# Gated linear attention with an ELU feed-forward on one core: low halves of four weight chunks by subtraction instead of matrix products, with a new start order

## The chip, the cores and the metric

The kernel runs on one core of a Trainium2 chip. The metric is the device time of one execution in microseconds (us). The engines have the names of the profile: PE (TensorE matmul), PEld (its weight load), DVE (VectorE), ACT (ScalarE), POOL (GpSimd) and SP (SyncE, which issues the loads).

## The reference

A gated linear attention runs over 4 batches x 8 heads, 768 steps, head size 48; its output is a 3072 x 384 matrix `x`, and a feed-forward with an ELU between two matrix products follows:

```python
state = alpha[t][:, None] * state + outer(k[t], v[t])
y[t]  = q[t] @ state
h = x @ w_in                     # 384 -> 2048
g = where(h > 0, h, exp(min(h, 0)) - 1)
out = g @ w_out                  # 2048 -> 384
```

The weights reach the kernel as float64, everything else as float32.

## The kernel before

**Precision.** The feed-forward's products run on pairs: each operand is kept as a rounded high part and a low part (the value less its high part), and three products (high x high, high x low, low x high) are added up in PSUM. So every weight has to be decoded, rounded (high) and subtracted (low) before it is used.

**Tiling.** Time is cut into 24 windows of 128 steps (6 to a batch), the feed-forward into 12 blocks of 256 rows (block `b` needs windows `2b` and `2b+1`) and 8 column groups `j` of 256. A weight chunk `f` is 128 x 768: `f = 2j` belongs to `w_in`, `f = 2j + 1` to `w_out`. Two chunks are decoded together as a pair `p`: chunks 0 and 2 are pair 0, 1 and 3 pair 1, 4 and 6 pair 2, 5 and 7 pair 3, and so on.

**The order.** Each piece of work is a token, a function of the same name. Two strings are walked from left to right, and each token's instructions go to the ends of their engines' queues: `START` (lines 49 to 76), which takes the kernel through the decode of all weights and up to the third column group of the feed-forward's last `O` of block 3, and `STEADY` (lines 79 to 86), which `steady()` unrolls from there. The engines run their own queues in order and wait for each other by semaphores. There is no planner at run time: what stands in the string is what each engine gets.

Tokens of a window `i`:

- `L`, `LA`, `LB`, `LV`: loads of keys, queries and decays, and of values (SP).
- `SC` (DVE scan of the decays, line 202), `LN`, `EX`, `PC` (ACT, lines 211, 216, 238), `KA`, `KB` (DVE or POOL by the tables `KAV`, `KBV`, lines 224, 229), `KC` (DVE, line 234): scaled keys. `SQ` (DVE or POOL by `SQV`, lines 251, 254): scaled queries.
- `TP` (PE transposes, line 275), `KN` (ACT copy, line 305), `S` (PE scores, line 340, from window 6 on line 324), `MK` (DVE mask), `U` and `UP` (PE, lines 387, 369, 413), `UA`, `UB`, `UC` (ACT or DVE: the state), `YL`, `Y3`, `Y` (PE, ACT, PE: the output, lines 448, 481, 493), `XH`, `XP`, `XL`, `XD`: high and low part of `x` (`XP`, for windows 0 to 2, lets PE form the rest; line 512). `ZV` is a clearing of a state buffer on POOL (line 268). `X` issues two idle products that only keep PE occupied (line 126).

Tokens of the weights: `F.f` (load, line 563), `KW.p` (ACT, line 572), `DA.p` and `DB.p` (DVE, lines 586, 591) decode a pair; `WH.f` (ACT, line 618) writes the high part. The low part is made in one of two ways. Where `f` is in the table `WPE`, `WP.f` lets PE copy the weight into PSUM by a product with the identity and take the high part off by a product with minus the identity, and `WL.f` is two ACT copies from PSUM; otherwise `WL.f` is one subtraction, on DVE where `f` is in `WLV`, else on POOL:

```python
nc.tensor.matmul(t, lhsT=ident, rhs=wm[p][:, k, c], start=True, stop=False, ...)   # WP, line 627
rest(t, wgts[f][:, 0, c])                                                          # WP, line 512
nc.scalar.copy(out=wgts[f][:, 1, h * DM:h * DM + DM], in_=t)                       # WL, line 636
eng(WLV, f).tensor_tensor(out=wgts[f][:, 1], in0=wm[p][:, k], in1=..., op=ALU.subtract)  # WL, line 638
```

`LC`, `CA`, `CB` check a weight chunk's range and are needed only at the end.

Tokens of the feed-forward: `A.b.j` (PE, 18 products, line 654; needs `WL.2j` and the `x` of block `b`), `RA`, `RB` (ACT, lines 662, 667), `RC` (DVE, line 673), `GH` (ACT, line 679), `GL` (DVE, or POOL by the table `GQS`, line 693), `O.b.j` (PE, 12 products, line 707; needs `WL.2j+1` and `GL.b.j`), `Z.b` (copy out and store).

Of the kernel before, what the change touches and what calls it, by code (L numbers as in the profile page):

```python
# [45 lines left out]
START = """
X.2.2 LA.0 SC.0 LN.0 LB.0 EX.0 KA.0 KB.0 LA.1 SC.1 KC.0 LN.1 LB.1 EX.1 SQ.1 KA.1 KB.1 TP.0 SQ.0 KC.1 S.0 PC.0 MK.0 F.2  # L50
LV.0 KN.0 U.0 UC.0 TP.1 F.0 UA.0 S.1 LV.1 LV.3 KN.1 KW.0 DA.0 DB.0 U.1 UP.1 UA.1 MK.1 YL.0 Y3.0 X.2.0 PC.1 L.2 UC.1
L.3 YL.1 SC.2 WH.0 LN.2 Y.0 SQ.2 Y3.1 XH.0 EX.2 WH.2 WP.0 F.6 Y.1 SC.3 WL.0 KA.2 KB.2 F.4 KC.2 WP.2 TP.2 XH.1 LN.3
PC.2 XP.1 KN.2 KW.2 DA.2 XP.0 DB.2 XL.0 XL.1 S.2 WL.2 EX.3 WH.6 LV.2 U.2 WH.4 UA.2 KA.3 MK.2 F.1 A.0.0 RA.0.0 A.0.1
RA.0.1 RB.0.1 UB.2 UC.2 WP.4 F.10 SQ.3 F.5 KB.3 KC.3 L.4 SC.4 RB.0.0 S.3 F.7 KW.3 DA.3 YL.2 TP.3 WL.4 LN.4 EX.4 KN.3
RC.0.1 MK.3 KA.4 WP.6 U.3 F.3 KW.1 DA.1 GH.0.1 Y3.2 Y.2 XH.2 SQ.4 RC.0.0 GH.0.0 KB.4 UA.3 UB.3 WL.6 YL.3 Y3.3 A.0.2
KC.4 TP.4 KN.4 F.9 RA.0.2 RB.0.2 DB.1 F.8 L.5 WH.1 DB.3 LC.0 WH.3 WL.3 A.0.3 F.14 XP.2 XL.2 LV.4 PC.4 WL.1 Y.3 RC.0.2
GL.0.0 XH.3 GL.0.1 XL.3 UC.3 GH.0.2 U.4 S.4 UA.4 MK.4 A.1.0 RA.1.0 KW.4 DA.4 A.1.3 RA.0.3 DB.4 RA.1.3 A.1.2 WH.7
RB.0.3 RB.1.3 WH.5 WL.5 GL.0.2 RB.1.0 WH.10 CA.0 RC.0.3 GH.0.3 RA.1.2 WH.8 WL.8 L.6 UB.4 UC.4 WL.10 RB.1.2 SC.5 LN.5
RC.1.0 GH.1.0 RC.1.3 A.1.1 RC.1.2 WL.7 F.12 PC.3 GL.0.3 EX.5 F.11 GL.1.0 RA.1.1 RB.1.1 O.0.0 L.7 O.0.1 RC.1.1 GH.1.2
GL.1.2 LC.1 CB.0 KA.5 KB.5 KW.5 DA.5 DB.5 GH.1.3 GH.1.1 O.0.2 A.0.5 A.0.4 O.0.3 RA.0.5 RB.0.5 O.1.0 LV.6 LV.5 RA.0.4  # L60
RB.0.4 GL.1.3 KC.5 A.1.4 A.1.5 WH.9 KW.6 DA.6 DB.6 GL.1.1 RA.1.4 RB.1.4 RC.1.4 O.1.1 GH.1.4 O.1.2 O.1.3 CA.1 WH.11
WH.14 WH.12 WL.12 TP.5 F.13 GL.1.4 WL.9 SQ.5 PC.5 RC.0.4 O.1.4 RC.0.5 RA.1.5 RB.1.5 KN.5 GH.0.5 S.5 Y.4 GH.0.4 RC.1.5
GH.1.5 GL.1.5 ZV.6 SC.6 WL.11 U.5 LN.6 MK.5 CB.1 GL.0.4 A.0.6 UA.5 EX.6 RA.0.6 WL.14 A.0.7 F.15 RB.0.6 RA.0.7 XH.4
RB.0.7 RC.0.6 KA.6 KB.6 KC.6 GH.0.6 SC.7 LN.7 EX.7 O.0.4 Y.5 TP.6 A.1.7 GL.0.6 XH.5 RC.0.7 GL.0.5 A.1.6 L.8 XL.4 XL.5
RA.1.7 RB.1.7 KW.7 DA.7 RA.1.6 O.0.5 LV.7 DB.7 RB.1.6 WH.15 KA.7 KB.7 KN.6 RC.1.7 KC.7 GH.0.7 O.1.5 WH.13 WL.15 U.6
UA.6 WL.13 PC.6 RC.1.6 GL.0.7 TA.7 XD.4 XD.5 LV.8 TB.7 A.2.3 A.2.0 RA.2.3 RB.2.3 GH.1.6 GL.1.6 UB.6 O.0.6 O.0.7 SQ.7
UC.6 SQ.6 GH.1.7 GL.1.7 Z.0 O.1.6 O.1.7 Z.1 SC.8 LN.8 S.7 RC.2.3 S.6 L.9 MK.7 U.7 UA.7 RA.2.0 A.2.1 A.2.5 EX.8 Y.7
RA.2.1 RB.2.1 RB.2.0 MK.6 PC.7 XH.7 Y.6 RC.2.0 KA.8 KB.8 UB.7 XH.6 UC.7 RC.2.1 GH.2.0 GH.2.1 A.2.2 XL.7 A.2.4 XD.7
GL.2.1 KC.8 SC.9 LN.9 RA.2.2 RB.2.2 LV.9 EX.9 RA.2.4 A.2.6 SQ.9 XL.6 XD.6 RC.2.2 RB.2.4 KA.9 GL.2.0 TA.8 KB.9 RA.2.6
A.2.7 KC.9 PC.8 GH.2.3 RB.2.6 RA.2.5 GL.2.3 RB.2.5 GH.2.2 RA.2.7 RB.2.7 RC.2.4 GH.2.4 A.3.0 RC.2.6 GH.2.6 RA.3.0  # L70
GL.2.2 TB.8 RB.3.0 RC.2.7 O.2.0 O.2.1 O.2.2 GL.2.6 O.2.3 RC.2.5 U.8 SQ.8 S.8 TP.9 GL.2.4 GH.2.7 RC.3.0 KN.9 UA.8 A.3.1
RA.3.1 GL.2.7 UB.8 UC.8 PC.9 O.2.4 GH.2.5 L.10 S.9 SC.10 U.9 RB.3.1 LN.10 MK.8 LC.2 UA.9 UB.9 EX.10 UC.9 MK.9 KA.10
A.3.4 KB.10 RA.3.4 RB.3.4 CA.2 L.11 A.3.2 GL.2.5 KC.10 SC.11 LN.11 EX.11 A.3.3 GH.3.0 RC.3.4 GL.3.0 RA.3.2 RB.3.2
KA.11 RA.3.3 LV.11 RC.3.1 KB.11 SQ.11 L.12 GH.3.1 TA.10 RB.3.3 RC.3.2 GH.3.2 GL.3.1 LV.10 GL.3.2 GH.3.4 RC.3.3 GH.3.3
GL.3.4 O.2.5 O.2.6 O.2.7 TB.10 CB.2 KC.11 LC.3 CA.3 Z.2 GL.3.3 O.3.0 TB.11 CB.3 SQ.10 PC.10 O.3.1 TA.11 LC.4 O.3.2
"""


# [895 lines left out]
```

## Time and profile before

| | us |
|---|---|
| median of 3 runs | 482.83 |
| lowest, highest | 481.2, 484.01 |
| the profiled execution, its own time | 483.17 |
| its span, first to last instruction | 481.5 |
| PE busy | 469.7 |
| DVE, ACT, POOL busy | 365.6, 317.4, 126.8 |

The execution's time is the span and 1.7 us around it. An engine's busy time is the time in which at least one of its instructions ran; PE's matmuls overlap, so that the distance of two starts, not the duration of one, is what an instruction costs there. Times in the rows are from the span's start.

### The profile page before, as it was taken

What the parts mean: (1) busy time and instruction counts of PE and PEld (TensorE: products, weight loads), DVE (VectorE), ACT (ScalarE), POOL (GpSimd) and SP (SyncE); (2) the same over time, 40 slices, a digit from 0 to 9 for tenths busy, and PEclk for the clock granted to TensorE, in tenths of its full rate; (3) what the DMA queues carried; (4) which work ended last, traced back from release to release, by engine and by line L of the source; (5) the groups of instructions that cost most, each with busy time, mean ns of one, the idle gap of its engine ahead of it and who ended that gap; (6) DMA issues with size and microseconds to landing.
All of it is one profiled execution on the core that took longest, in us unless ns stands there. A gap on an engine that the chain in (4) does not pass through costs nothing.

```text
span 481.5 us, 13214 instructions
## 1 busy us (share of the span) xinstructions
PE 469.7 (98%) x5438; PEld 451.2 (94%) x5438; DVE 365.6 (76%) x762; ACT 317.4 (66%) x672; POOL 126.8 (26%) x111
## 2 busy tenths in 40 slices
...
GB/s 303 416 417 413 95 1 99 24 249 10 135 148 101 100 34 164 150 108 167 106 128 148 106 105 174 102 132 120 132 132 147 39 124 56 44 66 10 2 35 37
DMA packets 20483, 61.13 MB, mean 127 GB/s; under 512 B 2880, under 2 KB 7872, under 8 KB 20416
## 3 DMA queue, kind: packets, MB, share of 16 engines
...
q14 instruction: 22, 0.18, 0.1%
HBM read 53.52 MB, written 4.72 MB: 121 GB/s over the span
## 4 chain that ended last, share of the span: by engine, by line
PE 79%; ACT 1%; DVE 1%; issue 0%; POOL 0%; POOLq 0%; DVEq 0%; ACTq 0%
PE h L654 35%; PE o L707 35%; PE y L453 4%; PE q L324 2%; PE q L369 2%; PE y L448 1%; ACT raw L572 0%; DVE wm L591 0%; POOL gl L693 0%; ACT r L662 0%; PE sc L340 0%; DVE w L638 0%; ACT w L618 0%; DVE r L673 0%; ACT r L667 0%
## 5 line engine op out<-in xcount | busy, mean ns | idle before, releaser
L654 PE MATMUL h<-xt,w 128*128 128x256 f32 x1728 | 201.4, 276 | 0.9 <-ACT xt L532 0.7
L654 PEld LDWEIGHTS h<-xt,w 128*128 128x128 f32 x1728 | 196.9, 192 | 2.4 <-ACT xt L532 0.9
L707 PE MATMUL o<-w,gh 128*128 128x384 f32 x768 | 188.5, 327 | 0.0
L707 PEld LDWEIGHTS o<-w,gh 128*128 128x128 f32 x768 | 132.9, 189 | 0.8 <-DVE w L638 0.3
L707 PE MATMUL o<-w,gl 128*128 128x384 f32 x384 | 125.3, 326 | 0.0
L662 ACT ACTIVATE r<-h 128x512 f32<-128x512 f32 x96 | 56.3, 597 | 60.7 <-PE h L654 53.5
L285 DVE STREAM_TRANSPOSE kn<-qka 32x128 f32<-32x128 f32 x256 | 77.5, 303 | 4.0
L673 DVE SCALAR_TENSOR_TENSOR h<-r,h 128x512 f32<-128x512 f32 x79 | 53.5, 690 | 28.2 <-ACT r L667 27.9
L707 PEld LDWEIGHTS o<-w,gl 128*128 128x128 f32 x384 | 72.6, 189 | 0.1
L693 DVE TENSOR_TENSOR gl<-h,gh 128x512 fp32r<-128x512 f32 x79 | 53.9, 688 | 19.0 <-ACT gh L679 16.2
L679 ACT CAST gh<-h 128x512 fp32r<-128x512 f32 x79 | 45.8, 580 | 33.0 <-DVE h L673 19.7
L667 ACT ACTIVATE r<-r 128x512 f32<-128x512 f32 x96 | 60.4, 633 | 1.9
L224 POOL TENSOR_TENSOR qka<-qka,R 128x512 f32<-128x512 f32 x18 | 23.2, 1287 | 138.4 <-ACT R L216 85.5
L254 POOL TENSOR_TENSOR st<-qka,P 64x512 f32<-64x512 f32 x30 | 38.0, 1267 | 23.0 <-DVE P L202 9.6
L352 DVE TENSOR_TENSOR st<-q,mask 64x256 f32<-64x256 f32 x72 | 30.3, 421 | 8.1 <-PE q L324 6.8
L229 POOL TENSOR_TENSOR R<-P,R 128x512 f32<-128x512 f32 x20 | 24.4, 1221 | 37.5 <-DVE qka L224 36.2
L211 ACT ACTIVATE R<-P 128x512 f32<-128x512 f32 x24 | 15.1, 629 | 28.0 <-DVE P L202 28.0
L693 POOL TENSOR_TENSOR gl<-r,gh 128x512 fp32r<-128x512 f32 x17 | 24.4, 1442 | 25.3 <-ACT gh L679 22.1
L202 DVE TENSOR_TENSOR_SCAN P<-qka,first 128x516 f32<-128x516 f32 x24 | 29.4, 1224 | 1.0 <-DMA qka<-in_qka_dram 0.9
L604 ACT ACTIVATE ck<-ck,lim 128x384 int32<-128x384 int8 x32 | 24.0, 751 | 2.5 <-DMA ck<-in_wgt_dram 2.5
L609 ACT ACTIVATE ck<-ck,lim 128x384 f32<-128x384 int32 x32 | 23.1, 722 | 0.7
L453 PEld LDWEIGHTS y<-st,vs 128*64 128x64 f32 x576 | 17.8, 138 | 2.4 <-issue 2.0
...
## 6 DMA issues: line engine op xcount, KB each, us to landing
...
```

Source lines behind the costliest of these rows:

```text
L202: nc.vector.tensor_tensor_scan(out=P.rearrange("p n w -> p (n w)"), data0=t[:, 2 * NP * W:], data1=first.rearrange("p n w -> p (n w)"), in ...
L254: eng(SQV, i).tensor_tensor(out=st[r, a], in0=d["q"][r], in1=pw(i)[r], op=ALU.mult)
L285: nc.vector.transpose(out=kn[32 * t:32 * t + 32, :, 32 * g:32 * g + 32], in_=d["kt"][32 * g:32 * g + 32, :, 32 * t:32 * t + 32])
L352: nc.vector.tensor_tensor(out=d["st"][r, a, :, c * C:(c + 1) * C], in0=d["s4"][a][o], in1=mask[o].unsqueeze(1).broadcast_to([64, NP, C]), ...
L453: nc.tensor.matmul(out[64 * a:64 * a + m], lhsT=lhs(i, c, a)[:, n * D:n * D + m], rhs=d["st"][:, a, n, c * C:(c + 1) * C], start=start, st ...
L654: nc.tensor.matmul(h[:, f, :], lhsT=t[:, wi, ws], rhs=x[:, :, c, xi].rearrange("p a x -> p x a"), start=(f == 0 and k == 0), stop=(k == 8) ...
L662: nc.scalar.activation(out=r, in_=d["h"], func=AF.Relu, scale=-1.0)
L667: nc.scalar.activation(out=d["r"], in_=d["r"], func=AF.Exp, scale=-1.0)
L673: nc.vector.scalar_tensor_tensor(out=d["g"], in0=d["r"], scalar=-1.0, in1=d["h"], op0=ALU.add, op1=ALU.max)
L679: nc.scalar.copy(out=gh, in_=d["g"])
L693: q.tensor_tensor(out=gl, in0=d["g"], in1=d["gh"].bitcast(F32), op=ALU.subtract)
L707: nc.tensor.matmul(o[:, 0:DM], lhsT=gt[:, f, ms], rhs=t[:, wi, f * DM:f * DM + DM].rearrange("p (a x) -> p x a", a=2), start=(j == 0 and f ...
```

## The change

Three things are changed, all of them tables; no function is.

- `WPE`, the chunks whose low part PE makes, becomes empty: the four `WP` tokens go, and chunks 0, 2, 4 and 6 are subtracted like the others.
- `WLV`, `KAV`, `KBV`, `SQV`, which say what DVE takes over from POOL, are new. Of the 16 subtractions DVE now has 8 and POOL 8 (before: 7 on DVE, 5 on POOL, 4 by PE with ACT).
- `START` is written in another order. Apart from the four `WP` tokens it holds the same tokens, 534 of them. `STEADY` is the same.

```diff
-WLV, KAV, KBV, SQV = (1, 7, 9, 10, 11, 14, 15), (0, 1, 2, 3, 4, 7), (0, 1, 2, 6), (1, 2, 3, 5, 7, 10, 11)
+WLV, KAV, KBV, SQV = (0, 1, 5, 9, 11, 12, 13, 15), (0, 2, 8, 10, 11), (0, 1, 2, 7, 8, 9, 10, 11), (2, 5, 6, 9)
-WPE, XPE, GPE, UPE = (0, 2, 4, 6), (0, 1, 2), (), (1,)
+WPE, XPE, GPE, UPE = (), (0, 1, 2), (), (1,)
 START = """
-X.2.2 LA.0 SC.0 LN.0 LB.0 EX.0 KA.0 KB.0 LA.1 SC.1 KC.0 LN.1 LB.1 EX.1 SQ.1 KA.1 KB.1 TP.0 SQ.0 KC.1 S.0 PC.0 MK.0 F.2
+LA.0 SC.0 LA.1 LN.0 EX.0 SC.1 LN.1 LB.0 KA.0 LV.0 KB.0 SQ.0 LB.1 KC.0 EX.1 TP.0 KA.1 KB.1 KC.1 PC.0 L.2 X.2.2 S.0 MK.0
...
 """
```

PE, around the first products of the feed-forward (`w_292` and `w_421` are the weights of pairs 0 and 2, `spare_395` the decoded pair 2; `qka_135` and `qka_133` hold windows 2 and 3, `vs_120` the values of window 2). Before:

```order
L340 MATMUL sc<-st,qka_135 64x64 x16
L369 MATMUL q<-vs_120,kn 64x48 x16
L654 MATMUL h<-xt,w_292 128x256 x36
L627 MATMUL wd<-spare_395,ident 128x384
L512 MATMUL wd<-w_421,minus 128x384
...
L340 MATMUL sc<-st,qka_133 64x64 x16
L448 MATMUL yl<-st,vs_120 64x64 x8
L275 MATMUL tp<-ident,qka_133 128x128 x4
```

The same place in the change (`w_431` and `w_573` are the weights of pairs 0 and 2, `vs_121` the values of window 3):

```order
L448 MATMUL y<-st,vs_120 48x64 x24
L512 MATMUL y<-xt,minus 128x384
L275 MATMUL tp<-ident,qka_133 128x128 x4
L340 MATMUL sc<-st,qka_133 64x64 x16
L654 MATMUL h<-xt,w_431 128x256 x18
L512 MATMUL y<-xt,minus 128x384
L369 MATMUL q<-vs_121,kn 64x48 x16
L654 MATMUL h<-xt,w_431 128x256 x18
L448 MATMUL yl<-st,vs_121 64x64 x8
L654 MATMUL h<-xt,w_573 128x256 x18
```

Before, `A.0.0` and `A.0.1` stood together behind window 2's `U`, with the output of window 2 and all of window 3 behind them; now window 2's output and window 3's `TP` and `S` stand ahead of `A.0.0`, and `A.0.0`, `A.0.1` and `A.0.3` are each separated by pieces of window 3.

POOL, from its first scaled queries (line 251) on. Before:

```order
L251 TENSOR_TENSOR st<-qka_133,P 128x512
L229 TENSOR_TENSOR R<-P,R 128x512
L251 TENSOR_TENSOR st<-qka_134,P 128x512
L229 TENSOR_TENSOR R<-P,R 128x512
L638 TENSOR_TENSOR w_676<-spare_395,w_676 128x768
```

In the change:

```order
L251 TENSOR_TENSOR st<-qka_133,P 128x512
L224 TENSOR_TENSOR qka_134<-qka_134,R 128x512
L251 TENSOR_TENSOR st<-qka_134,P 128x512
L251 TENSOR_TENSOR st<-qka_133,P 128x512
L224 TENSOR_TENSOR qka_133<-qka_133,R 128x512
L229 TENSOR_TENSOR R<-P,R 128x512
L268 MEMSET vs_120 64x192 x2
L638 TENSOR_TENSOR w_431<-wm,w_431 128x768
L638 TENSOR_TENSOR w_573<-spare_464,w_573 128x768 x2
```

POOL now has scaled queries and keys of windows 0, 1 and 3 and then, behind a clearing of a buffer for window 6 (`ZV.6`), the low parts of chunk 2 (`w_431`) and of chunks 6 and 4 (`w_573`), on which `A.0.1`, `A.0.3` and `A.0.2` wait.

## Rows read from the trace of the kernel before

**Rows 1.** The page's first part: busy time and share of the span of each engine.

```profile
PE 469.7 (98%) x5438; PEld 451.2 (94%) x5438; DVE 365.6 (76%) x762; ACT 317.4 (66%) x672; POOL 126.8 (26%) x111
```

**Rows 2.** Busy time by stretch: length, PE, PEld, DVE, ACT, POOL, clock, DMA, GB/s.

```profile
176.10:212.00 35.90, 35.90 (x416) 35.31 (x418) 29.25 (x65) 26.21 (x59) 10.56 (x10) 1.00 0.46 139
212.00:247.90 35.90, 35.90 (x436) 35.32 (x434) 31.82 (x75) 25.58 (x59) 10.00 (x8) 1.00 0.42 128
```

**Rows 3.** The chain that ended last: start, us, what; the first `Y` of STEADY.

```profile
176.08 1.89 PE y L453 x58
```

**Rows 4.** Who PE waited for, 0 to 180 us: total, times, longest.

```profile
PE wp L126 <- DVE first L120: 2.1, 1, 2.1
PE q L369 <- ACT kn L305: 1.7, 2, 1.2
PE y L493 <- ACT y L481: 1.6, 1, 1.6
PE h L654 <- ACT xt L532: 0.7, 1, 0.7
PE tp L275 <- issue: 0.5, 1, 0.5
PE yl L448 <- DVE st L357: 0.4, 1, 0.4
```

**Rows 5.** PE in order of time, 20 to 25 us: `WP.0`, `Y.1`, `WP.2`.

```profile
20.89 0.91 PE L627 MATMUL wd<-wm,ident 128*128 128x384 f32 x2
...
22.73 0.87 PE L493 MATMUL y<-y,sel 64*64 64x128 f32 x12
...
24.93 0.91 PE L627 MATMUL wd<-wm,ident 128*128 128x384 f32 x2
```

**Rows 6.** PE in order of time, 9 to 47 us, pieces of it.

```profile
9.97 0.63 PE L275 MATMUL tp<-ident,qka 128*128 128x128 f32 x4 [0.53 <-issue]
...
30.19 4.17 PE L654 MATMUL h<-xt,w 128*128 128x256 f32 x35 [0.73 <-ACT xt L532]
...
35.94 1.15 PE L340 MATMUL sc<-st,qka 48*64 48x64 f32 x32
...
37.53 0.66 PE L275 MATMUL tp<-ident,qka 128*128 128x128 f32 x4
38.02 0.81 PE L627 MATMUL wd<-spare,ident 128*128 128x384 f32 x2
...
40.31 0.68 PE L369 MATMUL q<-vs,kn 64*64 64x48 f32 x32 [0.49 <-ACT kn L305]
42.55 1.54 PE L493 MATMUL y<-y,sel 64*64 64x128 f32 x12 [1.55 <-ACT y L481]
```

**Rows 7.** Busy time by stretch of 1 us, columns as in Rows 2.

```profile
42.00:43.00 1.00, 0.45 (x4) 0.46 (x6) 0.90 (x3) 0.49 (x2) 0.43 (x1) 0.71 1.01 408
43.00:44.00 1.00, 1.00 (x15) 0.99 (x13) 1.00 (x2) 0.00 (x0) 0.00 (x0) 0.50 1.07 414
...
45.00:46.00 1.00, 1.00 (x27) 1.00 (x25) 1.00 (x1) 0.00 (x0) 0.00 (x0) 0.59 1.01 418
```

**Rows 8.** Weight decode, groups by line: xcount, busy us, mean ns.

```profile
L572 ACT ACTIVATE raw<-raw 128x1536 int32<-128x1536 uint8 x8 | 15.3, 1908 | 0.0
...
L591 DVE SCALAR_TENSOR_TENSOR spare<-raw 128x1536 int32<-128x1536 int32 x4 | 7.8, 1958 | 7.5 <-ACT raw L572 7.5
...
L618 ACT CAST w<-spare 128x768 fp32r<-128x768 f32 x8 | 6.5, 834 | 0.0
```

**Rows 9.** Line 638, low parts by subtraction: ns min/median/max, first and last start.

```profile
L638 DVE TENSOR_TENSOR w<-spare,w x4: 933/954/1451, 52.0 to 93.0; 128x768 fp32r<-128x768 f32 x4
L638 POOL TENSOR_TENSOR w<-wm,w x3: 1822/1841/2534, 63.5 to 113.0; 128x768 fp32r<-128x768 f32 x3
```

**Rows 10.** DVE in order of time: `KA.2` and `KC.2`.

```profile
22.22 0.69 DVE L224 TENSOR_TENSOR qka<-qka,R 128x512 f32<-128x512 f32 x1 [0.40 <-ACT R L216]
...
23.67 0.69 DVE L234 SCALAR_TENSOR_TENSOR qka<-R,qka 128x512 f32<-128x512 f32 x1
```

More of the change, by code (lines that the diff above doesn't have):

```diff
@@ L51 @@
[L51 to L75, printed above, removed]
+LA.0 SC.0 LA.1 LN.0 EX.0 SC.1 LN.1 LB.0 KA.0 LV.0 KB.0 SQ.0 LB.1 KC.0 EX.1 TP.0 KA.1 KB.1 KC.1 PC.0 L.2 X.2.2 S.0 MK.0
@@ new lines @@
+F.0 LV.1 KN.0 U.0 UA.0 UC.0 TP.1 SC.2 SQ.2 KN.1 X.2.0 YL.0 Y3.0 F.2 LN.2 EX.2 PC.1 SQ.1 S.1 MK.1 L.3 U.1 UP.1 KW.0
+UA.1 Y.0 XH.0 UC.1 KA.2 KB.2 KC.2 TP.2 S.2 YL.1 LV.2 KN.2 U.2 Y3.1 SC.3 SQ.3 LN.3 EX.3 MK.2 F.6 UA.2 DA.0 PC.2 XP.0
+YL.2 Y3.2 F.4 KW.2 KA.3 Y.1 UB.2 XH.1 DB.0 WH.0 Y.2 DA.2 F.1 XP.1 F.3 XL.0 KB.3 KC.3 TP.3 S.3 WL.0 XL.1 DB.2 A.0.0
+ZV.6 UC.2 LV.3 L.4 WH.2 PC.3 XH.2 XP.2 KN.3 DA.1 U.3 WL.2 UA.3 UB.3 MK.3 F.10 A.0.1 WH.6 WL.6 WH.4 YL.3 A.0.3 KW.1 F.5
+SC.4 Y3.3 Y.3 RA.0.0 WL.4 LN.4 RA.0.1 XL.2 DB.1 WH.1 WL.1 RB.0.0 RC.0.0 WH.3 RA.0.3 WL.3 A.0.2 XH.3 XL.3 LV.4 A.1.1
```

20 lines of the change are left out of this document (added).

## The prediction

> **What bounds the kernel now.** I began with the page's busy times: PE is busy for 469.7 of 481.5 us, 98%, and the next engine, DVE, for 76% [rows 1]. An average hides where the other 2% lie, so I took busy time by stretch. From 176.1 us on, PE is busy for 35.90 of 35.90 us, twice running, at full clock [rows 2]; the reader is to see that this repeated part has no hole that a better order could fill. The chain of waits gives the place where it begins: 176.08 us, the first `Y` of STEADY [rows 3]. STEADY is the same in the change, so what lies behind that point, 481.5 - 176.08 = 305.4 us, stays, and the change is worth what it takes off the 176 us of START.
>
> START has three losses. First, PE's own extra work, the four `WP`. Second, PE's waits: leaving out the 2.1 us before the warm-up products, the larger ones add up to 1.7 + 1.6 + 0.7 + 0.5 + 0.4 = 4.9 us [rows 4]; all but one of 1.2 us for `KN` lie before 45 us. Third, the clock. After waits of 0.49 and 1.55 us close together [rows 6] the granted clock is 0.71 in the 43rd us, 0.50 in the next two, and 0.59 in the 46th [rows 7]: 1.2 instead of 2.4 GHz, 0.29 + 0.5 + 0.5 + 0.41 = 1.7 us lost. So START holds 4.9 + 1.7 = 6.6 us in which PE stood or ran slowly, and a little over 7 us of work that is not needed.
>
> **The change, part by part.**
>
> *The four `WP` go.* `WP.0` begins at 20.89 us and the next step at 22.73: 1.84 us [rows 5]. `WP.6` begins at 38.02 and ends where the next wait begins, 40.31 - 0.49 = 39.82: 1.80 us [rows 6]. Four times 1.8 makes 7.2 us of PE. PE has no other work to hide it under, so all of it comes off: **-7.2**.
>
> *Their work on ACT goes, and four subtractions come.* Eight ACT copies fall away. Chunk 0 becomes a subtraction on DVE, median 0.95 us, and chunks 2, 4 and 6 become subtractions on POOL, 1.84 us [rows 9]. Neither engine is the bound, so their length costs nothing unless PE waits for one; that is the question of order, next.
>
> *The order up to the first feed-forward product.* Now PE does windows 0 to 2 whole, and `TP` and `S` of window 3, before `A.0.0`. Could that starve it? I added up PE's steps ahead of `A.0.0`, each at the distance of starts that the same step has in the trace (`Y` 22.73 to 24.93, 2.2 us [rows 5]; `S` and `YL` together 35.94 to 37.53, 1.6 us; `TP` 0.5 us [rows 6]): about 19.7 us in all. The warm-up products end near 9.0 us, and keys of window 0 are then ready, because they no longer stand behind other windows' work on DVE; before, the first `TP` ran at 9.97 after 0.53 us of waiting [rows 6]. So PE could reach `A.0.0` at 9.0 + 19.7 = 28.7 us. One wait I can name: on DVE, `UC.1` stands ahead of `KA.2`, `KB.2` and `KC.2`, so these begin only when PE has done `UP.1`. They take 22.22 to 24.36, 2.1 us [rows 10], `UC.1` some 0.35 more, and PE has only `Y.0`, about 1.9 us, to do meanwhile: 0.6 us. That puts `A.0.0` at 29.3. Before, the same product (but for its first instruction) began at 30.19 [rows 6], with the `S`, `YL`, `TP` and `Y` of the third and fourth window still to do.
>
> *Are the weights there by 29.3?* The decode of a pair is `KW` 1.9 (ACT), `DB` 2.0 (DVE), `WH` 0.8 (ACT) [rows 8] and `WL` 0.95 (DVE) [rows 9], 5.7 us in a row with nothing between. Following each engine's queue from the start with such durations, `DB.0` ends on DVE near 25.6 us (behind window 2's keys, `UA.2` and `UB.2`), `WH.0` near 27.2 and `WL.0` near 28.2, 1.1 us before it is wanted. `WL.2`, on POOL behind `ZV.6` (which waits for `Y.2`, near 27.5), ends near 30.8 and is wanted at 31.9; `WL.6` near 33.3, wanted at 34.5; `WL.4` near 35.2, wanted at 38.7. So nothing waits here by this sum, but four margins are about 1 us. Further on, `A.1.1` and `O.0.0` come out just in time, at a wait of 0.1 us each. Behind `O.0.0` (near 43 us) I find margins of 2 us and more up to 75, one of 0.5 at `A.1.6` (for `WL.12` on DVE), and more than 5 later: DVE and ACT have fallen far enough behind in what is asked of them.
>
> *What PE still waits.* 0.6 + 0.1 + 0.1 = 0.8 us by name. Every hop between engines adds a little that I left out, and margins of 1 us will not all hold. The lower end is 0.8 us; the upper is as much as before, 4.9 + 1.7 = 6.6 us. I take 2.0, near the lower end, since PE has some 4.3 us more attention work (the 2.2 + 1.6 + 0.5 above) in hand ahead of the first weights, where before most of its waits lay.
>
> *Loads.* The first pair's second chunk is now the ninth load instead of the seventh. No PE wait on a load shows in the trace [rows 4], and the decode of pair 0 begins, by the sum above, on ACT's queue and not on the load; I cost this at nothing. Later, `F.9` stands in SP's queue behind `L.7`, which waits for `S.4` to give its buffer free (near 54 us); its decode is wanted some 6 us later, so a late `S.4` would be the first thing to make the weights late there.
>
> **Sum.** 483.17 - 7.2 (`WP`) - 4.9 (waits) - 1.7 (clock) + 2.0 (waits left) = 471.4 us against the profiled execution. That execution is 0.34 us above the median of the runs shown, so against the median I predict **471.0 us**.
>
> **What speaks against it.** More subtractions now run on POOL and DVE at the same time. POOL's took 1.82 to 2.53 us, and DVE's 0.93 to 1.45 [rows 9], so both have a slow form. The Trainium skill (GPSIMD Engine Reference, Specifications) says that the two engines share their interfaces to SBUF and get in each other's way where a DVE instruction has two SBUF inputs, as these subtractions have. By that rule these three subtractions would come near the slow end; the spread in the rows agrees with it, though no row by itself shows the cause.
>
> **The rivals.**
>
> 1. *POOL's three low parts come at the slow end.* `WL.2`, `WL.6` and `WL.4` at 2.53 instead of 1.84 us are 0.7 us later each, one behind the other, 2.1 in all [rows 9]. For it: the spread. Against it: the margins of about 1 us take up part, and `WL.4`'s is 3.5. If all of it reached PE: 471.0 + 2.1 = 473.1 us.
> 2. *The waits only move.* `WP` falls away and PE still stands or runs slowly for 6.6 us, because several of the 1 us margins fail and the clock falls once, as it did at 42 us [rows 7]: 482.83 - 7.2 = 475.6 us; with the slow subtractions on top 477.7. For it: an order with many margins of 1 us. Against it: waits of 0.73 and 0.53 us by themselves went by without a fall [rows 6].
> 3. *Low clock for long, slower than before.* Ahead of `A.0.0` PE now has 20 us of small steps, each behind a chain of ACT, DVE and POOL. If waits there add up to some 2 us as at 40 to 42.5 [rows 6] and the clock then stays at 0.50 as in rows 7, each us of it costs 0.5. The gain left by the forecast is 11.8 us; with 2 to 3 us of waits it is used up if the clock stays low for some 18 us, and the time passes 485.2 at about 23 us, the whole way from 20 to 43: 486 us. Against it: the one fall in the trace lasted under 4 us, since full work followed it.
> 4. *No change that can be measured.* The same with the clock low for 15 to 20 us, or the weights of pairs 2 to 5 late by several us behind `F.9`: 481 to 485 us.
>
> **How the numbers follow.** A measurement of this kernel can tell about 0.5%, 2.4 us, from no change. The forecast (to 472.5) has 0.60, the first rival (472.5 to 474.5) 0.15, the second (to 480.4) 0.18, the fourth 0.04, the third 0.03. Faster: 0.60 + 0.15 + 0.18 = 0.93; same 0.04; slower 0.03. The range: with no wait left at all, 482.83 - 7.2 - 6.6 = 469.0, and 1 us below for work that I may have priced too high, 468.0; upwards to the second rival's end, 477.5. Above it lie rivals 3 and 4 and a little of the second, about 1 in 10.
>
> **What would show it.** Right: no `wd` products; the chain's first `Y` of STEADY near 164 us and 305 us behind it; the first `A` near 29 to 30 us, the first `O` near 43 to 45 us; PE's waits before 165 us of 1 to 3 us besides the warm-up's; a clock of 1.00 between 40 and 46 us. The first rival shows as POOL line 638 above 2.2 us and as the releaser of waits on PE line 654; the second as PE waits of 4 us or more and a stretch of clock below 1; the third as such a stretch of over 15 us. I am wrong if PE's waits exceed 7 us, or if STEADY no longer takes 305 us, for instance because DVE enters it with work left over from START.

## The result and the profile after

The changed kernel takes **488.0 us** (median of 13 runs, 484.61 to 491.38), the kernel before 482.98 (13 runs beside it, 481.2 to 484.93). The ratio is 1.0097, with an interval of 1.0068 to 1.0126: slower by 1%, where 471.0 us, faster by 2.5%, was forecast. The profiled execution took 489.34 us, its span is 487.5. One run of experiment 3 (491.43 us) and one of experiment 11 (595.81 us) were in a slower state of the chip and count in no median or ratio below.

The products are gone (no `wd` in the trace; 5414 PE instructions in place of 5438), and PE's busy time hardly falls. DVE's rises by 15.6 us with the same number of instructions. The page's first part after, beside [rows 1]:

```profile
PE 468.6 (96%) x5414; PEld 449.9 (92%) x5414; DVE 381.2 (78%) x762; ACT 314.2 (64%) x664; POOL 141.6 (29%) x115
```

The chain of waits after has the first `Y` of STEADY 4.5 us later than [rows 3], in place of the 11.8 us earlier that were forecast. From there on the two traces agree: PE's last product ends 301.3 us behind this place in either. The profiled span is 6.0 us longer, not 4.5, because the stretch behind PE's last product, in which the last block is copied and stored, took 1.6 us more; it differs from profile to profile of all the kernels here (4.1 to 6.3 us), so the place of this `Y` is the steadier measure in what follows.

```profile
180.59 1.77 PE y L453 x54
```

Who PE waited for, 0 to 180 us, after (columns as in [rows 4]): without the warm-up's row, the rows of 0.5 us and more sum up to 10.6 us, against the 4.9 that the prediction added up.

```profile
PE tp L275 <- POOL qka L224: 3.2, 1, 3.2
PE tp L275 <- issue: 2.4, 2, 1.2
PE wp L126 <- DVE first L120: 2.1, 1, 2.1
PE h L654 <- DVE r L673: 1.7, 1, 1.7
PE y L453 <- DVE st L352: 1.0, 1, 1.0
PE q L369 <- ACT kn L305: 1.0, 1, 1.0
PE sc L340 <- DVE gl L693: 0.8, 1, 0.8
PE h L654 <- ACT xt L508: 0.5, 1, 0.5
```

PE in order of time after: the first `TP` at 12.20 instead of 9.97 [rows 6], the `TP` of the third and fourth window with a wait each, `A.0.0` at 38.53.

```profile
12.20 1.09 PE L275 MATMUL tp<-ident,qka 128*128 128x128 f32 x4 [3.18 <-POOL qka L224]
...
27.37 0.63 PE L275 MATMUL tp<-ident,qka 128*128 128x128 f32 x4 [1.12 <-issue]
36.90 0.63 PE L275 MATMUL tp<-ident,qka 128*128 128x128 f32 x4 [1.25 <-issue]
38.53 2.27 PE L654 MATMUL h<-xt,w 128*128 128x256 f32 x18
```

Behind the first of these waits the granted clock falls to the lower of its two levels, 1.2 GHz, and stays there for nine us while PE is busy again (busy time by stretch, columns as in [rows 2]): 8.80 us of work at 0.50 and one at 0.52 lose 4.4 + 0.5 = 4.9 us. Before, it was 1.7 us [rows 7].

```profile
12.00:21.00 9.00, 8.80 (x96) 6.73 (x98) 5.35 (x7) 2.31 (x6) 1.14 (x1) 0.50 0.77 288
...
21.00:22.00 1.00, 1.00 (x25) 1.00 (x24) 0.00 (x0) 0.97 (x3) 0.00 (x0) 0.52 0.98 393
22.00:23.00 1.00, 1.00 (x31) 0.88 (x30) 0.61 (x1) 1.00 (x5) 0.00 (x0) 1.00 1.01 411
```

Why the keys came late stands in the next two fences, DVE and POOL in order of time after. DVE stands 1.99 us for the second load of window 0 (`LB.0`, now issued behind `LA.1`). Then `KB.0`, `KC.0` and `KB.1` take 1.55 to 1.78 us, each begun while a POOL instruction is running, where `KA.0`, begun 0.05 us ahead of POOL's, and `KC.1`, alone, take 0.69 like their kind in [rows 10]. (The wait at `TP.0` is put down to POOL's `KA.1` above, which ends at 11.55; `TP.0` starts 0.10 us behind the end of `KC.0`.)

```profile
8.01 0.69 DVE L224 TENSOR_TENSOR qka<-qka,R 128x512 f32<-128x512 f32 x1 [1.99 <-DMA qka<-in_qka_dram]
8.73 1.55 DVE L229 TENSOR_TENSOR R<-P,R 128x512 f32<-128x512 f32 x1
10.32 1.78 DVE L234 SCALAR_TENSOR_TENSOR qka<-R,qka 128x512 f32<-128x512 f32 x1
12.02 1.67 DVE L229 TENSOR_TENSOR R<-P,R 128x512 f32<-128x512 f32 x1
13.72 0.69 DVE L234 SCALAR_TENSOR_TENSOR qka<-R,qka 128x512 f32<-128x512 f32 x1
```

```profile
8.06 1.68 POOL L251 TENSOR_TENSOR st<-qka,P 128x512 f32<-128x512 f32 x1 [4.47 <-DMA qka<-in_qka_dram]
10.29 1.26 POOL L224 TENSOR_TENSOR qka<-qka,R 128x512 f32<-128x512 f32 x1 [0.56 <-DMA qka<-in_qka_dram]
11.51 1.63 POOL L251 TENSOR_TENSOR st<-qka,P 128x512 f32<-128x512 f32 x1
28.55 1.18 POOL L251 TENSOR_TENSOR st<-qka,P 128x512 f32<-128x512 f32 x1 [15.40 <-DVE P L202]
```

The two fences together tell more than that DVE is slow beside POOL. The three slowed steps end at 10.28, 12.10 and 13.69 us, and the POOL steps under way as they began end at 9.74, 11.55 and 13.14: each ends 0.55 us behind POOL's. So what such a step loses is about the rest of POOL's step, whatever that is, and the one that begins first is not slowed: `KA.0` takes its 0.69 us, and it is POOL's step beside it that takes 1.68 in place of 1.18.

The decode step `DB` (line 591; ns min/median/max, then first and last start) is lengthened too: its median for pairs in `spare` is 3.4 us, where the mean was 1.96 in [rows 8].

```profile
L591 DVE SCALAR_TENSOR_TENSOR wm<-raw x4: 1773/2658/2760, 31.5 to 101.1; 128x1536 int32<-128x1536 int32 x4
L591 DVE SCALAR_TENSOR_TENSOR spare<-raw x4: 2005/3424/3806, 37.6 to 74.5; 128x1536 int32<-128x1536 int32 x4
```

So DVE becomes nearly full in the stretch from the first `A` to 80 us. By stretch, of the kernel before, then of the one after (DVE is the third engine): 36.71 of 49.81 us, 74%, and 38.13 of 41.47, 92%.

```profile
30.19:80.00 49.81, 47.77 (x566) 45.58 (x567) 36.71 (x48) 38.72 (x70) 16.20 (x10) 0.97 0.51 196
```

```profile
38.53:80.00 41.47, 38.99 (x437) 37.36 (x434) 38.13 (x38) 32.80 (x49) 22.43 (x14) 1.00 0.42 166
```

One more term is seen only when PE's groups by line are put side by side, up to the first `Y` of STEADY: the same 522 `A` products keep PE busy for 61.8 us before and 63.6 after, and 216 of the `O` products for 53.1 and 53.7.

```profile
L654 PE MATMUL h<-xt,w 128*128 128x256 f32 x522 | 61.8, 277 | 0.9 <-ACT xt L532 0.7 <-DVE r L673 0.2
```

```profile
L654 PE MATMUL h<-xt,w 128*128 128x256 f32 x522 | 63.6, 278 | 2.8 <-DVE r L673 1.7 <-ACT xt L508 0.5 <-DVE w L638 0.3
```

The account of the 4.5 us: products -7.2, waits 10.6 - 4.9 = +5.7, low clock 4.9 - 1.7 = +3.2, `A` and `O` +2.4; sum +4.1, so 0.4 us have no name. The `A` term goes with the order and not with the tables: the 522 products are busy for 61.7 to 61.9 us in the profiles of experiments 4, 5, 10 and 12, which keep the old order, and for 63.1 to 64.7 in 1, 2, 3, 6, 8, 9 and 11.

### The profile page after: what moved, and what is told of

Same layout as the page of the kernel before. It is cut to its first block, busy times and chain, and to the rows that moved or that the text cites. A ratio compares the mean times of both kernels' runs of the same rounds, so it can differ in the third digit from the quotient of the medians.

```text
span 487.5 us, 13159 instructions
## 1 busy us (share of the span) xinstructions
PE 468.6 (96%) x5414; PEld 449.9 (92%) x5414; DVE 381.2 (78%) x762; ACT 314.2 (64%) x664; POOL 141.6 (29%) x115
## 4 chain that ended last, share of the span: by engine, by line
PE 71%; DVE 1%; ACT 0%; issue 0%; ACTq 0%
PE o L707 32%; PE h L654 31%; PE y L453 4%; PE q L324 2%; PE q L369 1%; DVE R L229 0%; DVE P L202 0%; DVE r L673 0%; DVE st L352 0%; DVE qka L224 0%; ACT R L238 0%; ACT gh L679 0%; ACT ot L716 0%; PE tp L275 0%; ACT r L662 0%
## 5 line engine op out<-in xcount | busy, mean ns | idle before, releaser
L224 POOL TENSOR_TENSOR qka<-qka,R 128x512 f32<-128x512 f32 x19 | 25.9, 1361 | 128.8 <-ACT R L216 83.6
L254 POOL TENSOR_TENSOR st<-qka,P 64x512 f32<-64x512 f32 x32 | 41.1, 1285 | 23.1 <-issue 7.9
L693 POOL TENSOR_TENSOR gl<-r,gh 128x512 fp32r<-128x512 f32 x17 | 26.1, 1542 | 60.7 <-ACT gh L679 53.4
L229 POOL TENSOR_TENSOR R<-P,R 128x512 f32<-128x512 f32 x16 | 21.4, 1337 | 1.3
```

Source lines behind the costliest of these rows:

```text
L254: eng(SQV, i).tensor_tensor(out=st[r, a], in0=d["q"][r], in1=pw(i)[r], op=ALU.mult)
L693: q.tensor_tensor(out=gl, in0=d["g"], in1=d["gh"].bitcast(F32), op=ALU.subtract)
```

## The experiments

Experiments are named by their number in the table. Each version has its median, its ratio to runs of the kernel before that were made beside it (whose medians were 482.82 to 483.25 us), and the first `Y` of STEADY in its profiled execution (176.08 before, 180.59 after). A profile is of one execution, which can be a fast or a slow one of its kernel: that of 10 was the fastest of eight (477.55 us) and that of 7 the slowest of nine (491.39). So profiles tell where time goes, and medians what a version is worth.

| | first `Y` of STEADY | median | ratio, interval |
|---|---|---|---|
| 1 change, longer warm-up | 176.51 | 485.3 | 1.0050 (1.0023 to 1.0077) |
| 2 change, first load in place | 179.05 | 485.01 | 1.0033 (1.0008 to 1.0058) |
| 3 change, low parts on DVE | 179.75 | 486.22 | 1.0050 (1.0026 to 1.0074) |
| 4 old order, no products | 175.96 | 483.72 | 1.0010 (0.9987 to 1.0033) |
| 5 the same, all low parts on DVE | 173.06 | 481.94 | 0.9980 (0.9958 to 1.0001) |
| 6 change, fed early, early steps on DVE | 177.62 | 485.93 | 1.0055 (1.0031 to 1.0079) |
| 7 before, POOL kept busy | 182.22 | 487.54 | 1.0078 (1.0048 to 1.0108) |
| 8 change, fed early, its own tables | 177.61 | 482.11 | 0.9975 (0.9949 to 1.0002) |
| 9 the same, longer warm-up | 174.77 | 483.65 | 1.0016 (0.9997 to 1.0034) |
| 10 as 5, three small steps first | 170.37 | 479.66 | 0.9930 (0.9904 to 0.9956) |
| 11 as 9, two small steps first | 175.25 | 482.36 | 1.0018 (0.9991 to 1.0046) |
| 12 before, two small steps first | 172.96 | 480.24 | 0.9951 (0.9934 to 0.9968) |

My theory after the result was that the waits at the start and the clock behind them ate the gain; the rivals were that the slow decode did, or that the products had never cost anything.

**1. Is it the clock?** The change with 12 more warm-up products, so that PE doesn't stand before the first `TP`.

```diff
-WARM = 25
+WARM = 37
```

> The changed kernel with 37 instead of 25 warm-up products, so that PE is busy until about 12.3 us, when window 0's keys are ready. If the low clock between 11 and 21 us costs time by itself (clock theory), the granted clock is 1.00 there, the stretch from the first transpose to window 1's U shortens from 11.4 to about 7.5 us, the first feed-forward product comes near 34.5 instead of 38.5 us and the time is about 484. If that stretch is held by DVE, ACT and POOL anyway (feeding theory), the first product stays within 1 us of 38.5 and the time near 488.

The clock stays at 1.00 from 10 to 50 us, and every later place is 4.0 to 4.1 us earlier (first `Y` of STEADY 176.51), 0.5 of it at the first `TP` already. So the low clock of 12 to 22 us was worth some 3.5 us net of the profiled time, as its theory had it; the medians differ by 2.7. It isn't everything: `TP.2` now waits for 2.02 us and `TP.3` for 1.25, and the version is still slower than before.

**2. Is it the load?** The change with `LB.0` issued ahead of `LA.1`.

```diff
-LA.0 SC.0 LA.1 LN.0 EX.0 SC.1 LN.1 LB.0 KA.0 ...
+LA.0 SC.0 LB.0 LA.1 LN.0 EX.0 SC.1 LN.1 KA.0 ...
```

> The changed kernel with window 0's keys and queries loaded ahead of window 1's decays, as before the change. If the late load starts the loss at the beginning (late-start theory), KA.0 begins near 6.4 instead of 8.0 us, the first transpose near 10 instead of 12.2 us, PE's wait there falls from 3.2 to 1 us or less, the clock does not fall, and the time is 5 to 7 us less, about 482. If slow DVE steps beside POOL decide there too (port theory), the transpose comes at 11 us or later, the clock still falls, and the time is 486 to 488.

The first `TP` runs at 9.81 us after a wait of 0.49, so the load had cost some 2.4 us there, which I had costed at nothing. But the next wait takes its place: `TP.2` stands for 1.95 us at 21.73, the clock falls there instead (0.83 over 20 to 30 us), and 1.5 of the 4.5 us are won back in the profile. The median is 3.0 us lower, where 5 to 7 were expected.

**3. Is it the slow low parts on POOL?** The change with chunks 2, 4 and 6 subtracted on DVE.

```diff
-WLV = (0, 1, 5, 9, 11, 12, 13, 15)
+WLV = (0, 1, 2, 4, 5, 6, 9, 11, 12, 13, 15)
```

> The changed kernel with the low parts of chunks 2, 4 and 6 on DVE instead of POOL. Port theory: DVE's decode steps of line 591 (2.65 to 3.8 us in seven of eight) fall to about 2.0 us for pairs 2 and 1, where POOL then stands still, so that DVE ends earlier although it has three steps of 0.95 us more; the time is 2 to 4 us less, 484 to 486. If DVE's length of queue is what counts (load theory), it is 2 to 3 us more, 490 or over.

The median of `DB` into `spare` falls from 3424 to 1884 ns, POOL being idle beside most of them, yet STEADY begins only 0.8 us earlier and the median falls by 1.8, less than the 2 to 4 us expected: DVE now does the subtractions itself, and the start, with its wait and low clock, is as it was. The first rival of the prediction, waits for POOL's low parts, is out: after, PE waits for a low part only once, for 0.3 us and on DVE.

**4 and 5. What were the products worth?** The order of before without its `WP` tokens, its four low parts by subtraction: in 4 on POOL but for chunk 0, in 5 all on DVE.

```diff
-WLV = (1, 7, 9, 10, 11, 14, 15)
+WLV = (0, 1, 7, 9, 10, 11, 14, 15)
-WPE = (0, 2, 4, 6)
+WPE = ()
```

```diff
-WLV = (1, 7, 9, 10, 11, 14, 15)
+WLV = (0, 1, 2, 4, 6, 7, 9, 10, 11, 14, 15)
-WPE = (0, 2, 4, 6)
+WPE = ()
```

> The kernel before, with its own order, without the four WP: chunk 0 is subtracted on DVE, chunks 2, 4 and 6 on POOL, as in the change. If taking PE's four products off is worth what I summed (7.2 us), and the loss lies in the new order, the time is 476 to 478. If the subtractions on POOL slow DVE's decode down so far that PE waits for it (port theory), it is 480 to 484, with line 591 above 2.4 us wherever POOL runs line 638 beside it.

> The kernel before without the four WP, chunks 0, 2, 4 and 6 all subtracted on DVE, so that POOL is no busier than before. Port theory: KB.2 (line 229 on DVE, 2.18 us beside POOL's subtraction in the run with chunks on POOL) is back at 0.69, and KC.3 (2.31) at 0.69; window 2's transpose waits 1.7 instead of 3.2 us, S.3 not at all. But since PE's four products stood in time in which PE now waits for window 2's keys (cover theory), the time stays within 2 us of the kernel before, 481 to 484. If the products were worth what I summed, it is 476 to 478.

These runs settle most. With 7.2 us less PE work and the order unchanged, 4 begins STEADY at 175.96 in place of 176.08, and its median is no lower: nothing. Without the warm-up's, PE's waits up to 180 us sum up to 9.9 us in place of 5.5, and the clock is 0.83 from 20 to 30 us and 0.66 from 40 to 50, where it was 1.00 and 0.83: 5.1 us lost in place of 1.7. The two, 4.4 and 3.4 us, eat what was taken out. So, but for the contention named below, the products had kept PE from waiting, and had kept its clock up with that. PE in order of time in 4:

```profile
25.92 0.63 PE L275 MATMUL tp<-ident,qka 128*128 128x128 f32 x4 [3.21 <-issue]
35.60 1.15 PE L340 MATMUL sc<-st,qka 48*64 48x64 f32 x32 [1.49 <-issue]
39.29 0.68 PE L369 MATMUL q<-vs,kn 64*64 64x48 f32 x32 [1.47 <-ACT kn L305]
41.53 1.54 PE L493 MATMUL y<-y,sel 64*64 64x128 f32 x12 [1.56 <-ACT y L481]
```

The first is where `WP.0` and `WP.2` stood; before, `TP.2` came there without a wait:

```profile
26.66 0.60 PE L275 MATMUL tp<-ident,qka 128*128 128x128 f32 x4
```

1.5 us of its 3.21 are contention: `KB.2` takes 2.18 us beside POOL's new subtraction (DVE, then POOL, in 4), where it took 0.69 alone.

```profile
22.92 2.18 DVE L229 TENSOR_TENSOR R<-P,R 128x512 f32<-128x512 f32 x1
```

```profile
22.60 1.95 POOL L638 TENSOR_TENSOR w<-wm,w 128x768 fp32r<-128x768 f32 x1 [16.23 <-ACT w L618]
```

With the subtraction on DVE, in 5, this wait is 1.73 us, and 3.0 us are won in the profile, 1.3 in the medians (with an interval up to 1.0001). So 4.2 us or more of the 7.2 don't come off. Two things share them: waits that the products had covered, and DVE's new subtractions of 0.95 us, of which that of chunk 0 stands ahead of window 2's keys here. 10 and 12 below part them at this place.

**7. The contention by itself.** The kernel before with 20 POOL multiplications of 128 x 256 (the expectation calls them additions) that nobody reads, from 6.4 to 27.2 us; no other work changes.

```diff
-... TP.0 SQ.0 KC.1 ...
+... TP.0 SQ.0 IDLE.20 KC.1 ...
```

> The kernel before with 20 idle POOL additions of work (two SBUF inputs, 256 columns, some 0.65 us each, read by nobody) behind SQ.0, where POOL otherwise stands still from 7 to 32 us; nothing waits for them. Port theory: DVE's steps with two SBUF inputs (lines 229, 234, 251, 591) between 7 and 25 us take 1.4 to 2.5 times as long, those with a PSUM input (line 357) and the scan (line 202) stay, and the time is 2 to 6 us more. If POOL's work costs only by its own lateness (queue theory), nothing changes: 481 to 484.

POOL, then DVE in order of time (lines are 9 higher here: 238 is `KB`, 211 the scan, 366 the mask, 600 `DB`):

```profile
6.44 20.76 POOL L159 TENSOR_TENSOR spin<-first 128x256 f32<-128x256 f32 x20
```

```profile
12.08 1.09 DVE L233 TENSOR_TENSOR qka<-qka,R 128x512 f32<-128x512 f32 x1
13.21 0.98 DVE L238 TENSOR_TENSOR R<-P,R 128x512 f32<-128x512 f32 x1
14.22 0.98 DVE L243 SCALAR_TENSOR_TENSOR qka<-R,qka 128x512 f32<-128x512 f32 x1
15.13 0.68 DVE L366 TENSOR_TENSOR st<-sc,mask 128x512 f32<-128x512 f32 x1
...
22.71 1.57 DVE L211 TENSOR_TENSOR_SCAN P<-qka,first 128x516 f32<-128x516 f32 x1
...
28.89 0.69 DVE L238 TENSOR_TENSOR R<-P,R 128x512 f32<-128x512 f32 x1
```

Steps with two inputs from SBUF go from 0.69 to 0.98 and 1.09 us, the scan (which I expected to stay) from 1.23 to 1.57, `DB` from 1.76 to 2.09; the mask, with one input from PSUM, stays at 0.68, and once POOL is done `KB` takes 0.69 again. POOL's steps are shorter in this run, and so is what DVE loses to each. STEADY begins 6.1 us later and the median rises by 4.3 us, though no engine that PE waits for has more to do: the slower keys make PE wait for 1.7 and 1.1 us at the first two `TP` (the first starts at 11.23, 0.10 us behind the end of `KC.0`), and the clock is 0.76 and 0.73 over the next two stretches of 10 us. The rule of the Trainium skill that the prediction weighed (GPSIMD Engine Reference, Specifications: shared SBUF interfaces, contention where a DVE instruction has two SBUF inputs) agrees with these rows.

**6 and 8. The new order, fed early.** The change with the load of 2 and window 2's keys ahead of `UC.1`; in 6 also eight early steps taken from POOL to DVE, in 8 the change's own tables.

```diff
-UA.1 Y.0 XH.0 UC.1 KA.2 KB.2 KC.2 TP.2 ...
+UA.1 Y.0 XH.0 KA.2 KB.2 KC.2 UC.1 TP.2 ...
```

```diff
-WLV, KAV, KBV, SQV = (0, 1, 5, 9, 11, 12, 13, 15), (0, 2, 8, 10, 11), (0, 1, 2, 7, 8, 9, 10, 11), (2, 5, 6, 9)
+WLV, KAV, KBV, SQV = (0, 1, 2, 4, 5, 6, 9, 11, 12, 13, 15), (0, 1, 2, 3, 8, 10, 11), (0, 1, 2, 3, 7, 8, 9, 10, 11), (1, 2, 3, 5, 6, 9)
```

> The changed kernel with three mends: window 0's keys loaded first, UC.1 behind KA.2, KB.2, KC.2 on DVE, and every POOL step before 50 us that stands beside DVE's (SQ.1, KA.3, KB.3, SQ.3, the low parts of chunks 2, 4, 6) on DVE. Port theory: line 591 takes 1.75 to 2.0 us for the first three pairs, window 3's transpose does not wait, the first feed-forward product comes near 30 us (38.5 in the changed kernel) and the time is 476 to 480. If DVE's length of queue binds instead (load theory), the first product comes at 33 us or later and the time is 482 or more.

> As the kernel with three mends, but with the changed kernel's own tables, so that POOL keeps SQ.1, KA.1, SQ.3, KA.3, KB.3 and the low parts of chunks 2, 4, 6. Port theory: line 591 stays at 2.6 to 3.5 us for the first pairs, window 3's transpose waits about 1 us, the first product comes 2 to 4 us later than with the POOL steps on DVE, and the time is 2 to 4 us more, 480 to 484. Load theory: no later than that kernel, and no slower.

In 6 the first three `DB` take 1.75 to 1.88 us and `TP.2` doesn't wait. But `SQ.1`, now on DVE, stands behind the scan of window 2, and the second window's scores wait for it; a short fall of the clock follows. `A.0.0` begins at 34.48 and the median is 485.93: what was expected if the length of DVE's queue binds, and not the 30 us and 476 to 480 of the other theory.

```profile
16.62 1.15 PE L340 MATMUL sc<-st,qka 48*64 48x64 f32 x32 [2.07 <-DVE st L251]
```

In 8 the first three `DB` take 2.65 to 3.60 us again and `TP.3` waits for 1.00, as expected, but `A.0.0` comes only 0.9 us later than in 6 and STEADY begins at the same place, where 2 to 4 us more were expected. The profiled execution has a wait of 1.86 us at the first `TP` and a clock of 0.53 behind it (12 to 16 us). The median is 3.8 us below that of 6. The runs tell why these two measures part: each has its mean granted clock, and seven of the twelve runs of 8 have 0.999 or 1.000 and take 479.9 to 483.5 us, while its profiled execution had 0.993 and took 484.61; the runs of 6 have 0.989 to 0.996. So one and the same kernel has runs in which the clock falls and runs in which it doesn't; that it is the start in which they part isn't shown, since only one of them has a profile.

**9. The start made safe.** 8 with 33 warm-up products.

```diff
-WARM = 25
+WARM = 33
```

> The two-step order with the first load and window 2's keys moved forward and the change's own tables took 479.9 to 485.6 us, least where the granted clock of the whole run was 1.00 and most where it was 0.993, as in its profile, with a wait of 1.9 us ahead of the first TP and a clock of 0.50 behind it. Here its 25 warm-up products are 33. Clock theory: PE is busy up to the first TP, the clock stays at 1.00 up to 30 us, the lowest runs stay near 480.5 (the longer warm-up takes up to 0.8 us where the keys came early) and the highest vanish: median 481, none above 483.5. Rival (the spread comes from something later than the start): the spread of 480 to 485.6 us stays and the whole moves up by 0.8 us: median 483.

Half a hit. PE has no wait between 8 and 20 us and STEADY begins 2.8 us earlier than in 8's profile. But the median is 483.65 (482.3 to 485.96): the low runs of 8 are lost too, by more than the 0.8 us allowed, and in the profile the clock falls at another place (0.83 over 30 to 40 us). The clock alone doesn't explain it: the eight runs of 9 with 0.999 or 1.000 take 482.3 to 484.0 us; what costs them about 2 us against those of 8 is open. The run confirms one term of the prediction, see below, and shows what is left: `A.0.0` begins at 32.06 us, and from there to STEADY it still takes 142.7 us (142.1 in the change), with 4.7 us of waits behind 60 us on the way.

**10, 11 and 12. Is a short step queued behind a long one?** The waits that are left in 5 end with a short ACT or DVE step that stands behind a decode step in its queue. 10 is 5 with three of them put ahead; 12 is the kernel before, products kept, with the two of these moves that it can have; 11 is 9 with two moves at the waits of 63 and 78 us.

```diff
-WL.0 KA.2 KB.2 F.4 KC.2 TP.2 ... TP.3 WL.4 LN.4 EX.4 KN.3 ... F.3 KW.1 DA.1 GH.0.1 Y3.2
+KA.2 KB.2 F.4 KC.2 WL.0 TP.2 ... TP.3 KN.3 WL.4 LN.4 EX.4 ... F.3 Y3.2 KW.1 DA.1 GH.0.1
```

```diff
-TP.3 WL.4 LN.4 EX.4 KN.3 ... F.3 KW.1 DA.1 GH.0.1 Y3.2
+TP.3 KN.3 WL.4 LN.4 EX.4 ... F.3 Y3.2 KW.1 DA.1 GH.0.1
```

```diff
-WH.8 KN.4 F.9 WL.8 ... A.0.5 DB.6 WH.9 RB.0.4 RC.0.4 GL.1.1
+KN.4 WH.8 F.9 WL.8 ... A.0.5 RB.0.4 RC.0.4 DB.6 WH.9 GL.1.1
```

> Old order without products, all low parts on DVE, and three small steps taken out from behind decode steps: WL.0 behind KC.2 (DVE), KN.3 ahead of LN.4 and EX.4 (ACT), Y3.2 ahead of KW.1 and GH.0.1 (ACT). Queue theory (PE waits for a short step that stands behind a long decode step in the same queue): the waits of 1.73 us at TP.2, 1.73 at U.3 and 1.53 at Y.2 fall to under 0.9, 0.5 and 0.3, 3.5 us less, and the low clock of 40 to 50 us (0.83, 1.7 us lost) goes too: the first Y of STEADY from 173.06 to 168 to 169.5, median 477 to 479, faster than before by 1%. Rival (the chain from engine to engine sets the pace, waits only move): the waits come back at S.3, A.0.2 or A.0.3, the first Y of STEADY within 1 us of 173, median 481 to 482.5.

> The kernel before, its four products kept, with two of the three moves of the run before: KN.3 ahead of WL.4, LN.4 and EX.4, and Y3.2 ahead of KW.1 and GH.0.1 (ACT). Beside the version without products that has these moves (first Y of STEADY at 170.37, median 479.66) it tells what the products cost where less waiting is left to cover them. Step of the prediction (all 7.2 us of the products count): first Y of STEADY at 177, median near 487. Cover theory (the products fill time in which PE would wait, and the waits of 0.49 us at U.3 and 1.55 at Y.2 in the kernel before shrink by about 1 us with the low clock of 42 to 46 us, 1.7 us, behind them): first Y of STEADY at 173 to 175, median 480 to 482, so the products cost 1 to 3 us net and not 7.

> The 33 warm-up products with two small steps of the two-step order taken out from behind decode steps: KN.4 ahead of WH.8 (ACT), RB.0.4 and RC.0.4 ahead of DB.6 (ACT, DVE). Queue theory: the waits of 1.06 us at U.4 and 1.72 at the A behind the four O near 80 us fall to under 0.4 each; the first Y of STEADY comes 2 to 2.5 us earlier than in the version with 33 warm-up products alone, median 478.5 to 479.5. Rival (waits only move): DB.6 and WL.8 come later and PE waits for them instead; within 0.7 us of that version.

10 is faster than either kernel, 479.66 us, 0.7% below the kernel before, though less than the 477 to 479 expected. PE in order of time in 10 (`TP.2`, `S.3`, `U.3`, `Y.2`); in 5 these waits were 1.73, 1.25, 1.73 and 1.53 us:

```profile
24.05 0.63 PE L275 MATMUL tp<-ident,qka 128*128 128x128 f32 x4 [1.37 <-issue]
...
33.03 1.15 PE L340 MATMUL sc<-st,qka 48*64 48x64 f32 x32 [1.23 <-issue]
...
36.17 0.68 PE L369 MATMUL q<-vs,kn 64*64 64x48 f32 x32 [0.92 <-ACT kn L305]
37.61 0.87 PE L493 MATMUL y<-y,sel 64*64 64x128 f32 x12 [0.76 <-ACT y L481]
```

The three that were aimed at (all but `S.3`) shrink by 2 us and not by the 3.5 expected; `TP.2`'s hardly does, since window 2's keys now wait 0.40 us for ACT. With them goes the low clock of 40 to 50 us (0.83 in 5, 1.00 in 10), and STEADY begins 2.7 us earlier. 12 wins 3.1 us in the same way without touching a product, 480.24 us, with one `Y` wait of 0.62 us left of [rows 6]'s 1.55 and a clock of 1.00 from 42 to 46 us [rows 7]. Between 12 and 10 the products, their low parts on DVE and the third move make 2.6 us in the profile; the medians differ by 0.6. The reason stands in the rows: in 12, `TP.2`, `S.3` and `U.3` come right behind their `WP` without a wait (PE in order of time in 12),

```profile
26.19 0.60 PE L275 MATMUL tp<-ident,qka 128*128 128x128 f32 x4
...
35.46 1.15 PE L340 MATMUL sc<-st,qka 48*64 48x64 f32 x32
...
39.28 0.68 PE L369 MATMUL q<-vs,kn 64*64 64x48 f32 x32
```

and in 10, without the products, the same three wait for 1.37 + 1.23 + 0.92 = 3.5 us. At `TP.2` no subtraction stands ahead of the keys any more, so there it is cover alone; ahead of window 3's keys, for which `S.3` waits, DVE now has chunk 2's subtraction of 0.95 us, so that wait is in part its price.

11 is the rival's case by its profile: STEADY begins 0.5 us later than in 9, where 2 to 2.5 us earlier were expected, though the clock is 1.00 throughout, and the median is 1.3 us lower, which is not clear of noise. The waits of 1.07 and 1.75 us shrink to 0.36 and nothing, and two others come, 1.33 and 1.93 us, where 9 had none and 0.24 (PE in order of time in 11):

```profile
80.74 0.65 PE L275 MATMUL tp<-ident,qka 128*128 128x128 f32 x4 [1.33 <-DVE gl L693]
...
99.50 2.25 PE L654 MATMUL h<-xt,w 128*128 128x256 f32 x18 [1.93 <-DVE xt L534]
```

DVE is busy for 19.56 of the 20 us from 60 to 80 us in 11, and both new waits end with a DVE step. That one step put first makes another late where DVE is that full is likely, but not shown: in 10, where the moves pay, DVE is busy for 9.96 of the 10 us from 30 to 40 us, and the two moves there are ACT's.

## Why the prediction was wrong

*STEADY is not touched: right.* PE's last product ends 301.3 us behind the first `Y` of STEADY in both.

*"PE has no other work to hide it under, all of it comes off": the first step that failed.* It read "PE is busy" as "PE's work sets the end". The four `WP` stood at places where a window's keys, or ACT's copy of them (`KN`), weren't ready; taken out alone they are worth 0 us in the profile of experiment 4 and 3.0 in that of 5, and with one move 2.6 between 12 and 10. The medians put it at less: 0.8 us slower, and 1.3 and 0.6 faster. The rows of before could have told a part of it: without `WP.0` PE comes to window 2's `TP` at 24.93 - 1.84 = 23.1 us [rows 5], and DVE's keys of that window end at 24.36 [rows 10], so 1.3 of the 3.6 us of `WP.0` and `WP.2` are cover; in 10 the wait there is 1.37.

*"What PE still waits", 2.0 us, and no low clock: failed.* The waits were 10.6 us and the lost clock 4.9, where the sum had taken all of the old 4.9 and 1.7 off. The steps marked as failed here, above and below, are what made them.

*"About 19.7 us" of PE's steps ahead of `A.0.0`: right.* In 9, where the clock is 1.00 up to 30 us, the first `TP` starts at 10.62 us and `A.0.0` at 32.06; less the waits of 0.93 and 0.39 that is 20.1.

*The first `TP` at 9.0 us and loads that cost nothing: failed.* It ran at 12.20. The sum took window 0's keys as ready by then "because they no longer stand behind other windows' work on DVE", and didn't follow SP's queue, in which `LB.0` now stands behind `LA.1`; experiment 2 alone brings `TP.0` back to 9.81.

*Durations of DVE's steps: failed, with a sign that was in the text.* The prediction named contention between DVE and POOL and then charged it to POOL's three low parts, 2.1 us at most. It fell on DVE: 0.69 became 1.55 to 1.78 us for keys, 1.96 became up to 3.8 for `DB`. The means of [rows 8] came from a kernel in which POOL was idle beside all eight `DB`; in the change it works beside seven of them, and six of these, begun while POOL's step was running, take 2.65 to 3.81 us. The seventh began first and took 1.77. DVE's busy time rose by 15.6 us. POOL's eight low parts, by contrast, have medians of 1.84 and 2.31 us.

*"Behind `O.0.0` margins of 2 us and more": failed.* DVE at 92% up to 80 us has no such margins; the waits of 0.8, 1.0, 1.7 and 0.3 us lie there, and 11 shows that they come back at other DVE steps when steps change places. That DVE's load makes them is likely; a version with less work for DVE there wasn't run.

*The rivals.* The second (waits only move) had the mechanism of the first failure, with a price of 4.6 to 6.7 us that took the products' 7.2 as gained. The third had the sign, the mechanism (waits of 2 to 3 us, then a clock of 0.50) and nearly the time, 486, and had a chance of 0.03. Its fall came at 12 us and not at 20, and lasted 10 us, not 23; the rest of the loss was the cover and DVE. It was judged by the one fall in the trace of before, said to be short because full work followed. The rows of before don't bear that out: small steps of window 2 and 3 followed, and the clock was up again by 46 us, before the next `A` began (busy time by stretch, columns as in [rows 2], then PE in order of time, before).

```profile
46.00:47.00 1.00, 1.00 (x30) 0.93 (x26) 0.65 (x1) 0.60 (x3) 0.00 (x0) 1.00 0.99 405
```

```profile
43.88 2.48 PE L448 MATMUL y<-st,vs 48*48 48x64 f32 x48
...
46.77 2.27 PE L654 MATMUL h<-xt,w 128*128 128x256 f32 x18
```

Why the fall of the change lasted three times as long isn't shown.

What stays open: the 2.4 us by which the same `A` and `O` products keep PE busy for longer in the new order, and after which waits the clock falls: those of 3.18 us in the change and 3.17 in 3 were followed by a fall, and so were 1.95 in 2 and 1.86 in 8, while 2.02 us in 1 was not.
